# A hardware loop for TensorE's head groups, fixed ring slots, and the last V half in two pieces

## The chip, the cores and the metric

One Trainium2 chip, one core. The metric is the device time of one launch in microseconds, as the median of several runs. On this core most runs of one kernel agree within 0.3%. A ratio is the mean time of one kernel's runs over the mean of the other kernel's runs of the same rounds on the same chip. It is therefore not quite the ratio of the medians that stand beside it. The profile is one execution. Its span runs from the first to the last instruction and is 1.8 to 2.1 us shorter than the time of that run. One run's profile needn't be a median run: the profiled run of the kernel before took 357.92 us.

## The reference

One decode step with two branches that share one input row: grouped-query attention over a cache of 32,768 positions, and a SwiGLU feed-forward. A gate mixes the two.

```python
# x [1,1,512]; 32 query heads, 8 KV heads, head size 128, 32768 cached positions, all bf16
g = sigmoid((x * gate_w).sum(-1))
q = x @ wq                                   # 512 x 4096
scores = q @ k_cache^T * 128 ** -0.5         # k_cache 8 x 32768 x 128
a = (softmax(scores) @ v_cache) @ wo         # v_cache the same size, wo 4096 x 512
b = (silu(x @ w_gate) * (x @ w_up)) @ w_down # 512 x 1792, twice, and back
out = g * a + (1 - g) * b
```

K and V are 64 MiB each. With the weights, 148 MB have to be read, and each byte is used once.

## The kernel before

SP (SyncE) streams everything through a ring of five 4 MB slots in SBUF. Each K or V half of a head group (16,384 positions x 128) is one transfer. Entry i of the stream goes into slot i mod 5, so SP waits until entry i - 5 has been used.

```python
stream = [("wq",), ("K", 0, 0), ("F1",), ("K", 0, 1), ("F2",)]
for g in range(1, G):
    for hf in range(2):
        stream += [("K", g, hf), ("V", g - 1, hf)]
stream += [("V", G - 1, 0), ("V", G - 1, 1), ("wo",)]
place = {e: i for i, e in enumerate(stream)}        # slot = place % 5
...
for i, e in enumerate(stream):                      # SP
    if i >= NSLOT:
        sp.wait_ge(*released[stream[i - NSLOT]])
    ...
        sp.dma_start(dst, src).then_inc(sem_ld[i], 16)
```

PE (TensorE) transposes K tile by tile, as pairs of bf16 read as one fp32. DVE (VectorE) copies every tile from PSUM to SBUF, and PE then multiplies it with q. The maximum, the exponentials and the transposed probabilities follow, and P·V of the group before. PE's program is written out for all eight groups, about 5,300 instructions. All semaphores count upward through the whole kernel.

```python
for e in stream[:-1]:                               # PE
    if e[0] == "K":
        pe.wait_ge(load_sem(e), 16)
        for q in range(FPH):                        # 16 tiles per half
            emit_fill(filled, kv_slot(e), q); filled += 1
            if filled >= NCG * (scored + 1) + 2:
                emit_scores(scored); scored += 1
            ...                                     # transposed P, and O of an earlier group
        continue
    ...
    pe.wait_ge(load_sem(e), 16)
    emit_pv(g, hf, kv_slot(e))
```

DVE's program is written out as well. Its main loop issues up to two waits before each of the 256 tile copies:

```python
for j in range(NF):                                 # DVE, NF = 256
    dve.wait_ge(sem_fill, j + 1)
    if j >= NKT:                                    # NKT = 8 tile buffers, NCG = 4 tiles per score block
        dve.wait_ge(sem_sc, (j - NKT) // NCG + 1)
    dve.tensor_copy(ktT[:, j % NKT, :], pst[j % NST]).then_inc(sem_cp, 1)
    ...
```

After the last V half the tail runs: P·V, a copy, four small matmuls (`osel`; the profile records each as two), scaling, a transposition, and the product with `wo`. `wo` is loaded last, in pieces of 2, 1, 0.5 and 0.5 MB.

## Time and profile before

| | before |
|---|---|
| median time | 357.1 us (later rounds on other chips: 357.4) |
| span of the profiled run | 356.1 us |
| PE / DVE / ACT busy | 72% / 56% / 4% |
| DMA share from 37 to 343 us | 1.00, at 429 GB/s |
| last landing of the last V half / of wo | 342.60 / 352.45 us |

The table by stretches of the kernel before; PEld is PE loading weights, ACT is ScalarE, POOL is GpSimd; the last three columns are the granted PE clock, the DMA share and GB/s:

```profile
core 0: us, PE busy (x) PEld busy (x) DVE busy (x) ACT busy (x) POOL busy (x), PEclk, DMA share, GB/s
37.00:343.00 306.00, 229.68 (x2212) 167.84 (x2214) 180.62 (x324) 13.03 (x34) 2.98 (x8) 0.86 1.00 429
343.00:357.00 14.00, 8.90 (x169) 6.04 (x161) 1.63 (x5) 0.00 (x0) 0.00 (x0) 0.50 0.36 149
```

DMA has no free time between 37 and 343 us, while PE is busy 230 of 306 us. The view of waits agrees: engine, line, whom it waited for; then us in total, times, longest.

```profile
PE ps L415 <- DMA ring<-in_A_k_cache_dram: 59.0, 14, 5.8
PE ps L431 <- DVE ktT L722: 15.1, 16, 0.9
```

PE stands still for K 14 times, up to 5.8 us each. The DMA queues of the page (packets, MB, share of the time of 16 DMA engines):

```profile
q1 hardware_dynamic: 5768, 148.11, 97.2%
q8 instruction: 20, 0.33, 0.4%
q14 instruction: 5, 0.04, 0.0%
```

The page lists q8 and q14 as `instruction` queues: 20 packets of 16 KB and 5 of 8 KB. The records below fit program code of PE and DVE that is fetched piece by piece by some of the DMA engines that also carry K and V, and are read so here. **A transfer lands when the slowest of its sixteen engines is done**: for the last V half the sixteenth update comes at 342.60 us, and PE starts at 342.65. The trace records the semaphore update of each engine for each transfer. Sorted, and with the first one subtracted, they give each engine's distance behind the fastest, in us. These rows are computed from those records; the records don't name the DMA engine:

```
kernel before, 4 MB transfers; first landing at: the sixteen distances
 22.18: 0 .04 .11 .12 .15 .16 .22 .28 .31  .35  .43  .97  1.17 1.20 1.59 1.80
122.51: 0 .05 .20 .28 .34 .94 1.12 1.16 1.50 1.60 1.61 1.67 1.67 1.76 1.84 3.53
229.33: 0 .04 .17 .35 .94 1.13 1.17 1.61 1.68 1.80 3.04 3.15 3.22 3.28 3.38 4.51
326.44: 0 .06 .16 .35 .96 1.16 1.19 3.06 3.11 3.17 3.22 3.23 3.30 4.83 4.95 6.45
```

The fastest engine needs 9.71 us per 4 MB half, from first to last. Eight engines step back one after the other by about 1.45 us, as often as q8 has a packet (16 KB, 1.0 to 1.1 us each). One other engine steps back by about 0.97 us right after each packet of q14 (8 KB; at 50.8, 111.2, 174.1, 243.1 and 307.2 us) and is 6.45 us behind at the end. The q8 packets start every 253 recorded PE instructions on average, those of q14 every 127 recorded DVE instructions. So they are taken for PE's and DVE's programs. The bytes alone, at the 27 GB/s that one engine makes in this stream (4 MB in 9.71 us by sixteen), would be an estimated 0.6 and 0.3 us.

The tail in the chain that ended last (start, us, what):

```profile
342.65 3.62 PE ps L463 x31
346.35 0.70 DVE pv_sb L715
347.09 1.88 PE ps L479 x8
349.98 3.61 PE ps L542 x128
353.73 0.35 DVE res L765
```

### The profile page before, as it was taken

The numbers are of one execution on the slowest core, as the hardware profiler recorded it, in microseconds if no ns is written. First come the engines' busy times: TensorE is split into PE (matmuls) and PEld (weight loads), VectorE is DVE, ScalarE is ACT, GpSimd is POOL, SyncE is SP. The second block draws the span as 40 slices with busy tenths as digits, with TensorE's granted clock in tenths as the row PEclk, the third lists the DMA queues.
The fourth block names the chain that finished last, engine by engine and source line by source line (L and its number), as shares of the span: only waits on it lengthen the run. The fifth ranks groups of instructions, "written<-read, shape, count | busy, mean of one in ns | idle before, by whom it ended". The sixth has DMA issues, their size and how long they took to land.

```text
span 356.1 us, 6079 instructions
## 1 busy us (share of the span) xinstructions
PE 255.3 (72%) x2615; PEld 187.4 (53%) x2615; DVE 197.9 (56%) x371; ACT 14.5 (4%) x36; POOL 5.6 (2%) x22
## 2 busy tenths in 40 slices
PE   0439998849497947858395959778495949577746
PEld 0436885647384726546283838464473728274415
DVE  1239198828266845848183756657282838457401
ACT  1000101000100010000100010000100010000000
POOL 0200000000000000000000000000000000000000
PEclk9999789969859996989789798989698898989555
DMA  8999999999999999999999999999999999999991
GB/s 339 420 405 466 416 431 418 445 429 420 436 438 415 434 436 423 432 438 421 432 436 427 431 429 434 429 421 439 431 418 443 431 414 445 430 420 438 425 380 64
DMA packets 5797, 148.49 MB, mean 417 GB/s; under 512 B 650, under 2 KB 652, under 8 KB 908
## 3 DMA queue, kind: packets, MB, share of 16 engines
q1 hardware_dynamic: 5768, 148.11, 97.2%
q8 instruction: 20, 0.33, 0.4%
q14 instruction: 5, 0.04, 0.0%
q10 hardware_dynamic: 4, 0.00, 0.0%
HBM read 148.11 MB, written 0.00 MB: 416 GB/s over the span
## 4 chain that ended last, share of the span: by engine, by line
DMA 66%; PE 29%; DVE 3%; issue 2%; POOL 0%; SPq 0%; DVEq 0%
DMA ring<-in_A_k_cache_dram 56%; PE ps L415 17%; DMA ring<-in_A_v_cache_dram 10%; PE ps L431 5%; PE ps L463 3%; PE ps L384 2%; DVE ktT L722 2%; PE ps L479 1%; PE ps L542 1%; PE ps L445 0%; DVE pv_sb L715 0%; DVE pmaxf L678 0%; POOL gmax L288 0%; SPq L298 0%; DVE res L765 0%
## 5 line engine op out<-in xcount | busy, mean ns | idle before, releaser
L722 DVE COPY ktT<-ps 128x1024 bf16<-128x1024 bf16 x256 | 163.6, 683 | 104.7 <-PE ps L415 102.0
L415 PE MATMUL ps<-ident_f,ring 128*128 128x128 f32 x1024 | 161.3, 316 | 59.8 <-DMA ring<-in_A_k_cache_dram 59.0
L415 PEld LDWEIGHTS ps<-ident_f,ring 128*128 128x128 f32 x1024 | 136.9, 164 | 93.7 <-DMA ring<-in_A_k_cache_dram 65.7
L431 PE MATMUL ps<-ktT,qz 128*32 128x512 bf16 x512 | 42.1, 406 | 15.2 <-DVE ktT L722 15.1
L463 PE MATMUL ps<-ring,ET 128*16 128x512 bf16 x512 | 33.8, 410 | 5.7 <-DMA ring<-in_A_v_cache_dram 5.5
L463 PEld LDWEIGHTS ps<-ring,ET 128*16 128x16 bf16 x512 | 13.2, 94 | 22.4 <-DMA ring<-in_A_v_cache_dram 5.9
L431 PEld LDWEIGHTS ps<-ktT,qz 128*32 128x32 bf16 x512 | 7.9, 95 | 28.3 <-DVE ktT L722 24.3
L569 ACT ACTIVATE P<-ps,nbias 128x512 bf16<-128x512 f32 x16 | 10.8, 682 | 273.4 <-DVE nbias L699 273.4
L678 DVE TENSOR_REDUCE pmaxf<-ps 128x1 f32<-128x512 f32 x16 | 11.1, 692 | 11.9 <-PE ps L431 11.9
L479 PEld LDWEIGHTS ps<-osel,pv_sb 128*128 128x128 f32 x64 | 11.0, 258 | 2.1 <-DVE pv_sb L715 2.1
L479 PE MATMUL ps<-osel,pv_sb 128*128 128x4 f32 x64 | 10.7, 291 | 1.0 <-DVE pv_sb L715 0.9
L715 DVE COPY pv_sb<-ps 128x512 f32<-128x512 f32 x8 | 5.5, 682 | 8.9 <-PE ps L463 8.9
L288 POOL PARTITION_ALL_REDUCE gmax<-pmax x8 | 3.0, 373 | 310.2 <-DVE pmax L688 310.2
L445 PE MATMUL ps<-ident,P 128*128 128x128 bf16 x64 | 6.2, 219 | 1.8 <-ACT P L569 1.2
L707 DVE COPY ET<-ps 128x512 bf16<-128x512 bf16 x16 | 6.6, 413 | 1.3 <-PE ps L445 1.3
L384 PEld LDWEIGHTS ps<-xT,ring 128*128 128x128 bf16 x112 | 6.8, 159 | 0.4 <-issue 0.4
L384 PE MATMUL ps<-xT,ring 128*128 128x1 bf16 x112 | 6.9, 198 | 0.0
L359 PE MATMUL ps<-xT,ring 128*128 128x1 bf16 x128 | 3.5, 165 | 4.5 <-DMA ring<-in_A_wq_dram 4.5
L445 PEld LDWEIGHTS ps<-ident,P 128*128 128x128 bf16 x64 | 4.8, 98 | 2.6 <-ACT P L569 2.4
L342 PE MATMUL ps<-ones_bf,x_row 1*128 1x1 bf16 x4 | 0.3, 171 | 7.8 <-DMA gw_row<-in_gate_w_dram 7.8
L359 PEld LDWEIGHTS ps<-xT,ring 128*128 128x128 bf16 x128 | 3.5, 104 | 4.5 <-issue 4.5
L342 PEld LDWEIGHTS ps<-ones_bf,x_row 1*128 1x128 bf16 x4 | 0.2, 112 | 7.8 <-DMA gw_row<-in_gate_w_dram 7.8
(67 smaller groups left out, 36.5 us busy)
## 6 DMA issues: line engine op xcount, KB each, us to landing
ring<-in_A_k_cache_dram SPq DMA_DIRECT2D x16, 4096.0 KB, 43.1
ring<-in_A_v_cache_dram SPq DMA_DIRECT2D x16, 4096.0 KB, 37.1
ring<-in_A_wq_dram SPq DMA_DIRECT2D x1, 4096.0 KB, 13.2
ring<-in_A_wo_dram SPq DMA_DIRECT2D x1, 2048.0 KB, 38.8
ring<-in_B_w_gate_dram SPq DMA_DIRECT2D x1, 1792.0 KB, 26.6
ring<-in_B_w_up_dram SPq DMA_DIRECT2D x1, 1792.0 KB, 30.5
ring<-in_B_w_down_dram SPq DMA_DIRECT2D x1, 1792.0 KB, 43.5
ring<-in_A_wo_dram SPq DMA_DIRECT2D x1, 1024.0 KB, 40.8
```

What stands on the lines that cost most here:

```text
L359: ins = pe.matmul(ps_m[:, M_Q0 + h : M_Q0 + h + 1], wq_v[:, c, h * DH : (h + 1) * DH], xT[:, c : c + 1], start=(c == 0), stop=(c == KC - 1),)
L384: ins = pe.matmul(ps_m[:, base + j : base + j + 1], wt[:, c, :].rearrange("d (p j) -> d j p", j=FC)[:, j, :], xT[:, c : c + 1], start=(c = ...
L415: ins = pe.transpose(stb[:, t * 64 : (t + 2) * 64], two.bitcast(FP32), ident_f[:, :])
L431: ins = pe.matmul(ps_sc[f % NSC][32 * c : 32 * c + 32, :], qz[:, g, e, 24 - PB * i : 56 - PB * i], kt[:, e, :], start=(i == 0 and e == 0), ...
L445: ins = pe.transpose(ps_pt[:, (f % 2) * 512 + m * 128 : (f % 2) * 512 + (m + 1) * 128], P[:, f % 2, m * 128 : (m + 1) * 128], ident[:, :],)
L463: ins = pe.matmul(ps_pv[32 * c : 32 * c + 2 * PB, :], ET[:, f % NET, col : col + 2 * PB], src.rearrange("p (i c t) d -> p i c t d", i=NI, ...
L479: ins = pe.matmul(ps_m[:, M_OT + g * HPG : M_OT + (g + 1) * HPG], pv_sb[:, r * DH : (r + 1) * DH], osel[:, r * HPG : (r + 1) * HPG], start ...
L569: act.activation(P[:, f % 2, :], ps_sc[f % NSC], ACT.Exp, bias=nbias[:, f // 2 : f // 2 + 1], scale=SCALE, accum_out=esum[:, f // 2, f % 2 ...
L678: ins = dve.tensor_reduce(pmaxf[:, f : f + 1], ps_sc[f % NSC], AX.X, ALU.max)
L707: dve.tensor_copy(ET[:, f % NET, :], ps_pt[:, (f % 2) * 512 : (f % 2 + 1) * 512]).then_inc(sem_ptc, 1)
L715: dve.tensor_copy(pv_sb[:, :], ps_pv).then_inc(sem_pvc, 1)
L722: dve.tensor_copy(ktT[:, j % NKT, :], pst[j % NST]).then_inc(sem_cp, 1)
```

## The change

Its intent: PE's groups 1 to 7 become one hardware loop, so that its program shrinks, from 5,302 recorded instructions to about 2,020. The loop is written with the same addresses and the same semaphore values in every turn. So K and V halves get fixed slots (four rotate, the fifth holds F2 and later wo), q of the group is copied to one place (`qc`), O of a group is copied out of one PSUM place, and PE subtracts from its semaphores what it has waited for. Besides, the last V half comes as two transfers, so that half of its P·V can run earlier. Cut to its core:

```diff
-    place = {e: i for i, e in enumerate(stream)}
+    place = {("wq",): 1, ("F1",): 3, ("F2",): 4, ("wo",): 4}
+    for g in range(G):
+        for hf in range(2):
+            place["K", g, hf] = 2 * hf
+            place["V", g, hf] = 2 * hf + 1
...   # SP
-                    if i >= NSLOT:
-                        sp.wait_ge(*released[stream[i - NSLOT]])
+                    if e in before:                 # the entry before in the same slot
+                        sp.wait_ge(*released[before[e]])
...
+                        if e == ("V", G - 1, 1):
+                            sp.dma_start(dst[:, : RH // 2, :], src[:, : RH // 2, :]).then_inc(ld, 16)
+                            sp.dma_start(dst[:, RH // 2 :, :], src[:, RH // 2 :, :]).then_inc(sem_ldv, 16)
...   # PE
+                def take(sem, n):
+                    pe.wait_ge(sem, n)
+                    pe.sem_inc(sem, -n)
...
-                for e in stream[:-1]:               # everything written out
-                    ...
+                pe.wait_ge(sem_bpre, 1)
+                with pe.Fori(1, G):
+                    emit_k(0)
+                    emit_pv(0)
+                    emit_k(1)
+                    emit_pv(1)
+                    pe.sem_inc(sem_exp, -2)
+                    pe.sem_inc(sem_ptc, -2)
+                    pe.sem_inc(sem_qc, -1)
...
+                emit_pv(1, halves=True)             # P.V of the first piece, wait for sem_ldv, the rest
...   # DVE: one q copy and one copy of O per group
+                dve.tensor_copy(qc[:, :, :], qz[:, g, :, :]).then_inc(sem_qc, 1)
+                dve.tensor_copy(oT[:, g * HPG : (g + 1) * HPG], ps_m[:, M_OT : M_OT + HPG]).then_inc(sem_oc, 1)
```

More of the change, by code (lines that the diff above doesn't have):

```diff
@@ L71, in bass_gated_mix__gqa_block_cached__swiglu_ffn__decode_kernel @@
     stream += [("V", G - 1, 0), ("V", G - 1, 1), ("wo",)]
-    place = {e: i for i, e in enumerate(stream)}
+    place = {("wq",): 1, ("F1",): 3, ("F2",): 4, ("wo",): 4}
[3 more added lines that the diff above has]
+            place["V", g, hf] = 2 * hf + 1
+    before = {}
+    for i, e in enumerate(stream):
+        for d in stream[:i]:
+            if place[d] == place[e]:
+                before[e] = d
     with ExitStack() as es:
@@ L80, in T @@
             return es.enter_context(nc.sbuf_tensor(name, shape, dt))
-        sem_ld = [S_(f"s_ld{i}") for i in range(len(stream) - 1)]
+        sem_ld = [S_(f"s_ld{i}") for i in range(NSLOT)]
+        sem_ldv = S_("s_ldv")
         sem_ldo = [S_(f"s_ldo{i}") for i in range(len(WO_CUT))]
@@ L122, in bass_gated_mix__gqa_block_cached__swiglu_ffn__decode_kernel @@
         sem_pt = S_("s_pt")
+        sem_qc = S_("s_qc")
+        sem_oc = S_("s_oc")
         sem_ptc = S_("s_ptc")
@@ L163, in bass_gated_mix__gqa_block_cached__swiglu_ffn__decode_kernel @@
         qz = T("qz", [128, G, 2, 56], BF16)
+        qc = T("qc", [128, 2, 56], BF16)
         sg = T("sg", [128, FC], FP32)
@@ L180, in bass_gated_mix__gqa_block_cached__swiglu_ffn__decode_kernel @@
         pv_sb = T("pv_sb", [128, 512], FP32)
+        oT = T("oT", [128, H], FP32)
         oTs = T("oTs", [128, H], BF16)
@@ L201, in bass_gated_mix__gqa_block_cached__swiglu_ffn__decode_kernel @@
         M_OT = M_B0
-        M_O0 = M_OT + H
+        M_O0 = M_OT + HPG
         M_BR = 256
@@ L209, in slot_of @@
         def slot_of(entry):
-            return ring[:, place[entry] % NSLOT, :]
+            return ring[:, place[entry], :]
         def kv_slot(entry):
@@ L294, in _ @@
                 for i, e in enumerate(stream):
-                    if i >= NSLOT:
-                        sp.wait_ge(*released[stream[i - NSLOT]])
+                    ld = sem_ld[place[e]]
+                    if e in before:
+                        sp.wait_ge(*released[before[e]])
                     if e[0] == "wq":
                         sp.dma_start(wq_v, A_wq.rearrange("(p c) n -> p c n", c=KC)).then_inc(
-                            sem_ld[i], 16
+                            ld, 16
                         )
@@ L302, in _ @@
                         sp.dma_start(wg, B_w_gate.rearrange("(p c) f -> p c f", c=KC)).then_inc(
-                            sem_ld[i], 16
+                            ld, 16
                         )
                         sp.dma_start(wu, B_w_up.rearrange("(p c) f -> p c f", c=KC)).then_inc(
-                            sem_ld[i], 16
+                            ld, 16
                         )
@@ L309, in _ @@
                         sp.dma_start(wd, B_w_down.rearrange("(p j) n -> p j n", j=FC)).then_inc(
-                            sem_ld[i], 16
+                            ld, 16
                         )
@@ L325, in _ @@
                         dst = kv_slot(e)
-                        sp.dma_start(dst, src).then_inc(sem_ld[i], 16)
+                        if e == ("V", G - 1, 1):
+                            sp.dma_start(dst[:, : RH // 2, :], src[:, : RH // 2, :]).then_inc(
+                                ld, 16
+                            )
+                            sp.dma_start(dst[:, RH // 2 :, :], src[:, RH // 2 :, :]).then_inc(
+                                sem_ldv, 16
+                            )
+                        else:
+                            sp.dma_start(dst, src).then_inc(ld, 16)
                 sp.wait_ge(sem_res, 1)
@@ L355, in emit_q @@
                 def emit_q():
-                    pe.wait_ge(load_sem(("wq",)), 16)
+                    take(load_sem(("wq",)), 16)
                     for h in range(H):
@@ L379, in emit_ffn @@
                 def emit_ffn():
-                    pe.wait_ge(load_sem(("F1",)), 32)
+                    take(load_sem(("F1",)), 32)
                     for base, wt in ((M_G0, wg), (M_U0, wu)):
@@ L393, in emit_outb @@
                 def emit_outb():
-                    pe.wait_ge(load_sem(("F2",)), 16)
+                    take(load_sem(("F2",)), 16)
                     pe.wait_ge(sem_tT, 1)
@@ L405, in emit_outb, with emit_fill @@
                     ins.then_inc(sem_pe_b, 1)
-                def emit_fill(j, src, q):
-                    if j >= NST:
-                        pe.wait_ge(sem_cp, j - NST + 1)
-                    stb = pst_f[j % NST]
+                def emit_fill(src, q):
+                    stb = pst_f[q % NST]
+                    if q >= NST:
+                        pe.wait_ge(sem_cp, q - NST + 1)
                     for t in range(0, TPF, 2):
@@ L418, in emit_fill, with emit_scores @@
                     ins.then_inc(sem_fill, 1)
-                def emit_scores(b):
-                    f, i = b // NI, b % NI
-                    g = f // 2
-                    if b == 0:
-                        pe.wait_ge(sem_qz, 4)
-                    if i == 0 and f >= NSC:
-                        pe.wait_ge(sem_exp, f - NSC + 1)
-                    pe.wait_ge(sem_cp, NCG * (b + 1))
+                def emit_scores(hf, i, first):
+                    if i == 0 and hf == 0:
+                        pe.wait_ge(sem_qc, 1)
+                    if i == 0 and not first:
+                        pe.wait_ge(sem_exp, hf + 1)
+                    pe.wait_ge(sem_cp, NCG * (i + 1))
                     for e in range(2):
                         for c in range(NCG):
-                            kt = ktT[:, (NCG * b + c) % NKT, :].rearrange("p (k e) -> p e k", e=2)
+                            kt = ktT[:, (NCG * i + c) % NKT, :].rearrange("p (k e) -> p e k", e=2)
                             ins = pe.matmul(
-                                ps_sc[f % NSC][32 * c : 32 * c + 32, :],
-                                qz[:, g, e, 24 - PB * i : 56 - PB * i],
+                                ps_sc[hf][32 * c : 32 * c + 32, :],
+                                qc[:, e, 24 - PB * i : 56 - PB * i],
                                 kt[:, e, :],
@@ L438, in emit_scores, with emit_k, emit_pt @@
                     ins.then_inc(sem_sc, 1)
-                def emit_pt(f):
-                    pe.wait_ge(sem_exp, f + 1)
-                    if f > 0:
-                        pe.wait_ge(sem_ptc, f)
+                def emit_k(hf, first=False):
+                    e = ("K", 0, hf)
+                    take(load_sem(e), 16)
+                    done = 0
+                    for q in range(FPH):
+                        emit_fill(kv_slot(e), q)
+                        if q + 1 >= NCG * (done + 1) + 2:
+                            emit_scores(hf, done, first)
+                            done += 1
+                        if q == NCG and hf == 0 and not first:
+                            emit_o()
+                        if q == FPH // 2 and not first:
+                            emit_pt(hf)
+                    while done < NI:
+                        emit_scores(hf, done, first)
+                        done += 1
+                    pe.sem_inc(sem_cp, -FPH)
+                def emit_pt(hf):
+                    pe.wait_ge(sem_exp, hf + 1)
                     for m in range(NM):
                         ins = pe.transpose(
-                            ps_pt[:, (f % 2) * 512 + m * 128 : (f % 2) * 512 + (m + 1) * 128],
-                            P[:, f % 2, m * 128 : (m + 1) * 128],
+                            ps_pt[:, hf * 512 + m * 128 : hf * 512 + (m + 1) * 128],
+                            P[:, hf, m * 128 : (m + 1) * 128],
                             ident[:, :],
@@ L450, in emit_pt, with emit_pv @@
                     ins.then_inc(sem_pt, 1)
-                def emit_pv(g, hf, src):
-                    f = 2 * g + hf
-                    if hf == 0 and g > 0:
-                        pe.wait_ge(sem_pvc, g)
-                    pe.wait_ge(sem_ptc, f + 1)
-                    for m in range(NM):
-                        for i0 in range(0, NI, 2):
+                def emit_pv(hf, halves=False):
+                    e = ("V", 0, hf)
+                    take(load_sem(e), 16)
+                    pe.wait_ge(sem_ptc, hf + 1)
+                    src = kv_slot(e).rearrange("p (i c t) d -> p i c t d", i=NI, c=NCG)
+                    for i0 in range(0, NI, 2):
+                        if i0 > 0 and halves:
+                            pe.wait_ge(sem_ldv, 16)
+                        for m in range(NM):
@@ L459, in emit_pv @@
                             for c in range(NCG):
                                 col = m * 128 + c * 32 + i0 * PB
-                                first = hf == 0 and m == 0 and i0 == 0
-                                last = hf == 1 and m == NM - 1 and i0 == NI - 2
                                 ins = pe.matmul(
                                     ps_pv[32 * c : 32 * c + 2 * PB, :],
-                                    ET[:, f % NET, col : col + 2 * PB],
-                                    src.rearrange("p (i c t) d -> p i c t d", i=NI, c=NCG)[
-                                        :, i0 : i0 + 2, c, 2 * m : 2 * m + 2, :
-                                    ].rearrange("p i t d -> p i (t d)"),
-                                    start=first,
-                                    stop=last,
+                                    ET[:, hf, col : col + 2 * PB],
@@ L471, in emit_pv, with emit_o @@
+                                    src[:, i0 : i0 + 2, c, 2 * m : 2 * m + 2, :].rearrange(
+                                        "p i t d -> p i (t d)"
+                                    ),
+                                    start=(hf == 0 and i0 == 0 and m == 0),
+                                    stop=(hf == 1 and i0 == NI - 2 and m == NM - 1),
                                 )
                     ins.then_inc(sem_pv, 1)
-                def emit_o(g):
-                    if g == 0:
-                        pe.wait_ge(sem_osel, 1)
-                    pe.wait_ge(sem_pvc, g + 1)
+                def emit_o():
+                    take(sem_pvc, 1)
+                    take(sem_oc, 1)
@@ L478, in emit_o @@
                     for r in range(NBLK):
                         ins = pe.matmul(
-                            ps_m[:, M_OT + g * HPG : M_OT + (g + 1) * HPG],
+                            ps_m[:, M_OT : M_OT + HPG],
                             pv_sb[:, r * DH : (r + 1) * DH],
@@ L490, in _ @@
                 pe.wait_ge(sem_ident, 2)
-                scored = 0
-                filled = 0
-                for e in stream[:-1]:
-                    if e[0] == "K":
-                        pe.wait_ge(load_sem(e), 16)
-                        for q in range(FPH):
-                            emit_fill(filled, kv_slot(e), q)
-                            filled += 1
-                            if filled >= NCG * (scored + 1) + 2:
-                                emit_scores(scored)
-                                scored += 1
-                            if e[1] >= 1 and q == FPH // 2:
-                                emit_pt(2 * (e[1] - 1) + e[2])
-                            if e[2] == 0 and e[1] >= 2 and q == NCG:
-                                emit_o(e[1] - 2)
-                        continue
-                    while scored * NCG < filled:
-                        emit_scores(scored)
-                        scored += 1
-                    if e[0] != "V":
-                        {"wq": emit_q, "F1": emit_ffn, "F2": emit_outb}[e[0]]()
-                        continue
-                    _, g, hf = e
-                    if e == ("V", G - 1, 0):
-                        emit_pt(2 * G - 2)
-                        emit_pt(2 * G - 1)
-                        emit_o(G - 2)
-                    if e == ("V", G - 1, 1):
-                        pe.wait_ge(sem_em, 1)
-                        pe.matmul(
-                            ps_e[:, 0:H],
-                            ones_f[:, :],
-                            em[:, :, :].rearrange("p g h -> p (g h)"),
-                            start=True,
-                            stop=True,
-                        ).then_inc(sem_pe_S, 1)
-                    pe.wait_ge(load_sem(e), 16)
-                    emit_pv(g, hf, kv_slot(e))
@@ L530, in _ @@
-                emit_o(G - 1)
+                pe.wait_ge(sem_osel, 1)
+                emit_q()
+                emit_k(0, first=True)
+                emit_ffn()
+                emit_k(1, first=True)
+                pe.sem_inc(sem_qc, -1)
+                emit_outb()
+                pe.wait_ge(sem_bpre, 1)
[6 more added lines that the diff above has]
+                    pe.sem_inc(sem_ptc, -2)
+                    pe.sem_inc(sem_qc, -1)
@@ new lines, in _ @@
+                emit_pt(0)
+                pe.wait_ge(sem_ptc, 1)
+                emit_pt(1)
+                emit_o()
+                emit_pv(0)
+                pe.wait_ge(sem_em, 1)
+                pe.matmul(
+                    ps_e[:, 0:H],
+                    ones_f[:, :],
+                    em[:, :, :].rearrange("p g h -> p (g h)"),
+                    start=True,
+                    stop=True,
+                ).then_inc(sem_pe_S, 1)
+                emit_pv(1, halves=True)
+                emit_o()
@@ L587, in _ @@
                 dve.memset(ps[:, 6:8, :], 0.0).then_inc(sem_pv0, 1)
+                dve.memset(pv_sb[:, :], 0.0).then_inc(sem_pvc, 1)
+                dve.memset(oT[:, :], 0.0).then_inc(sem_oc, 1)
                 dve.wait_ge(sem_pe_x, 1)
@@ L712, in emit_pvc, with emit_oc, emit_qc @@
                     dve.wait_ge(sem_pv, 2 * (g + 1))
-                    if g > 0:
-                        dve.wait_ge(sem_pe_o, g)
+                    dve.wait_ge(sem_pe_o, g + 1)
                     dve.tensor_copy(pv_sb[:, :], ps_pv).then_inc(sem_pvc, 1)
+                def emit_oc(g):
+                    dve.wait_ge(sem_pe_o, g + 2)
+                    dve.tensor_copy(
+                        oT[:, g * HPG : (g + 1) * HPG], ps_m[:, M_OT : M_OT + HPG]
+                    ).then_inc(sem_oc, 1)
+                def emit_qc(g):
+                    dve.tensor_copy(qc[:, :, :], qz[:, g, :, :]).then_inc(sem_qc, 1)
+                dve.wait_ge(sem_qz, 4)
+                emit_qc(0)
                 for j in range(NF):
@@ L721, in _ @@
                         dve.wait_ge(sem_sc, (j - NKT) // NCG + 1)
-                    dve.tensor_copy(ktT[:, j % NKT, :], pst[j % NST]).then_inc(sem_cp, 1)
+                    dve.tensor_copy(ktT[:, j % NKT, :], pst[q % NST]).then_inc(sem_cp, 1)
                     if j == FPH + 1:
                         emit_t()
-                    if j == 2 * FPH + 1:
-                        emit_bpre()
                     if q == FPH - 1:
@@ L729, in _ @@
                         if f % 2 == 1:
+                            if f < NH - 1:
+                                emit_qc(f // 2 + 1)
                             emit_nbias(f // 2)
@@ L732, in _ @@
                         emit_ptc(f - 2)
+                    if j == 2 * FPH - 1:
+                        emit_bpre()
                     if q == 1 and f >= 4 and f % 2 == 0:
                         emit_pvc(f // 2 - 2)
+                    if q == NCG + 2 and f == 2:
+                        dve.wait_ge(sem_pe_o, 1)
+                        dve.tensor_copy(oT[:, 0:HPG], ps_m[:, M_OT : M_OT + HPG]).then_inc(
+                            sem_oc, 1
+                        )
+                    if q == NCG + 2 and f >= 4 and f % 2 == 0:
+                        emit_oc(f // 2 - 2)
                 emit_ptc(2 * G - 2)
@@ L737, in _ @@
                 emit_ptc(2 * G - 1)
-                dve.wait_ge(sem_exp, NH)
+                emit_oc(G - 2)
                 dchain(
@@ L753, in _ @@
                 emit_pvc(G - 1)
-                dve.wait_ge(sem_pe_o, G)
-                dve.tensor_tensor(oTs[:, :], ps_m[:, M_OT : M_OT + H], rS[:, :], ALU.mult).then_inc(
-                    sem_oT1, 1
-                )
+                dchain(
+                    dve.tensor_tensor(
+                        oTs[:, 0 : H - HPG], oT[:, 0 : H - HPG], rS[:, 0 : H - HPG], ALU.mult
+                    )
+                )
+                dve.wait_ge(sem_pe_o, G + 1)
+                dve.tensor_tensor(
+                    oTs[:, H - HPG :], ps_m[:, M_OT : M_OT + HPG], rS[:, H - HPG :], ALU.mult
+                ).then_inc(sem_oT1, 1)
                 dve.wait_ge(sem_oT1, 1)
```

## The prediction

> **What bounds the kernel now.** The DMA stream. The table by stretches gives a DMA share of 0.98 to 1.01, about 430 GB/s, from 37 to 343 us. PE is busy 72%; between groups it waits for the next K half (waits: 59.0 us in 14 waits, longest 5.8). The trace's landing records (sixteen engines' updates per transfer) say more: the fastest engine finishes a 4 MB half every 9.71 us, while the slowest falls behind, from 1.4 us at the first landing to 6.4 at the last. The steps fit the instruction queues: each 16 KB fetch of PE's program (20 packets, queue q8) costs one engine about 1.45 us, rotating over eight engines, which end up to 4.95 us behind; five 8 KB fetches (q14, which fit DVE's program) all hit one other engine, 0.97 us each: 6.4 us behind. A transfer lands when its slowest engine is done: last V 342.6 us, last wo piece 352.45.
>
> **What the change does.**
> - Tail: in the chain, last V lands at 342.6, then 3.62 us of P·V, 0.70 copy, 1.88 osel matmuls, small steps, wo matmuls 349.98 to 353.6. In two pieces, half of the P·V runs before the last landing: an estimated 1.8 us less, so wo matmuls could start at 348.2. But the last wo piece lands at 352.45, and its 16 matmuls are an eighth of 3.61 us: wo ends at 352.95 instead of 353.6. Only about 0.65 us shows; the rest becomes waiting for wo.
> - Four ring slots rotate instead of five. K's next load is issued when K's transposes end, 10.3 us after landing, and needed 29.1 us after it (three transfers of 9.71): 18.8 us to spare: DMA does not starve. K's issue-to-landing time falls from 43.1 to about 28.5 us.
> - Added: a q copy per group, seven copies of O, a dummy osel product, a wait for b_pre before the loop: inside PE's 4 to 6 us of idle per K half.
> - The loop: about 560 PE instructions per turn[...]. [...] If the loop stays resident, 8 to 10 fetches remain, and PE's engines gain 1.5 to 3 us; but the last landing belongs to DVE's engine, so the time hardly changes. The bad case is refetches always on the same engines: seven on one, about 10.5 us behind, last landing 4 us later.
>
> **Predicted time: 356.7 us, 80% range 355.2 to 360.0.** Chances: faster by over 2% 0.02, within 2% 0.94, slower by over 2% 0.04.
>
> **Right or wrong in the profile.** Last V landing within 0.5 us of 342.6; half of its P·V before it; a wait for wo inside the last matmuls; K landing 28 to 29 us after issue; DMA share 1.00; [...]slowest engine still that of q14's fetches.
>
> **What would make it wrong.** Refetches piling on few engines; [...]a changed number of DVE fetches (0.97 us each).

The time comes to 357.1 us less about 0.4: 0.65 us gained in the tail, less an allowance for some chance of loss. An estimate: 8 to 10 fetches from about 2,020 recorded instructions at one packet per 253, and 10.5 us from seven steps of the measured 1.45 us on top of what an engine is behind at the start.

## The result, and the profile after

| | before | after |
|---|---|---|
| median | 357.1 us (4 runs) | 357.41 us (4 runs) |
| ratio | | 1.0008, 95% interval 0.9991 to 1.0026: the same |
| repeated later, on another chip | 357.47 (11 runs) | 357.29 (5 runs), ratio 0.9993 (0.9980 to 1.0006) |

The queues after:

```profile
q1 hardware_dynamic: 5912, 148.12, 97.3%
q8 instruction: 8, 0.13, 0.2%
q14 instruction: 5, 0.04, 0.0%
```

PE's fetches (q8) fall from 20 to 8; DVE's (q14) stay at five. The last of PE's before the tail ends at 92.6 us, just after the first turn of the loop; the next starts at 349.1. In between, six more turns run without one q8 packet, at 559 recorded PE instructions per turn, where the kernel before had one packet per 253. PE's six taken branches were recorded with 215 to 242 ns each, the one not taken with 83 ns. After each taken branch PE waits 4.3 to 7.7 us for its next K half, and the weight load of its first transposition starts 0.10 us after K has landed, in every turn, as it also does where the same turns are written out (pe_unrolled below). So whatever the branch costs is hidden in the wait for K.

And yet the kernel is no faster. The distances before the gap described below, and at the last V landing:

```
kernel after, first landing at: the sixteen distances
326.41: 0 .03 .10 .17 .18 .24 1.15 1.17 1.42 1.59 1.62 1.77 1.87 1.92 1.96 6.44
338.93: 0 .04 .06 .07 .09 .10 .11 .13 .14 .18 .19 .25 .28 .32 .40 3.71
```

The eight engines that carry PE's program are now at most 1.96 us behind, where they had been up to 4.95. The one that carries DVE's program is 6.44 behind, as before, and it alone sets the landing: 342.64 us instead of 342.60.

The table by stretches for the end, first of the kernel before, then of the kernel after:

```profile
326.00:334.00 8.00, 5.95 (x68) 3.45 (x64) 4.73 (x17) 1.45 (x4) 0.37 (x1) 0.80 0.98 420
```

```profile
326.00:334.00 8.00, 3.97 (x52) 2.18 (x44) 4.30 (x18) 1.45 (x4) 0.37 (x1) 0.93 0.83 328
```

Here the DMA share falls to 0.83, which the prediction had not seen coming. The last V half follows directly on another V half, so its slot (shared with the V half two entries earlier) is needed two transfers later, not four. It was issued at 327.2 us, and fifteen engines had run dry: the first of them finishes the first piece at 334.03 us (331.38 in the run without this gap, see the experiment with the spare slot). The slowest engine had work until 332.85 and lost nothing. That is why the distances shrink from 6.44 to 3.71 without anything getting earlier.

The tail in the timeline (start, us, engine, line, what; in brackets the idle time before and what ended it):

```profile
337.88 1.04 PE L505 MATMUL ps<-ring,ET 128*16 128x512 bf16 x16 [1.04 <-PEq L361]
342.68 1.89 PE L505 MATMUL ps<-ring,ET 128*16 128x512 bf16 x16 [3.76 <-DMA ring<-in_A_v_cache_dram]
348.57 3.46 PE L574 MATMUL ps<-ring,O 128*1 128x128 bf16 x112 [0.28 <-DVE O L819]
352.53 0.59 PE L574 MATMUL ps<-ring,O 128*1 128x128 bf16 x16 [0.50 <-DMA ring<-in_A_wo_dram]
353.30 0.35 DVE L823 SCALAR_TENSOR_TENSOR res<-ps,g_col,b_pre 128x128 bf16<-128x128 f32 x1 [4.78 <-PE ps L574]
```

Half of P·V is done before the last landing, the wo matmuls start at 348.57 instead of 349.98, and then they wait for the last piece of wo (landed 352.49). Of 1.41 us gained at the start, 0.43 is left at the last step (353.30 against 353.73).

A note on reading: after the change, waits for K are no longer listed under DMA. PE now waits in a semaphore instruction of its own, and the view names PE's sequencer:

```profile
PE ps L443 <- PEq L361: 52.1, 14, 6.8
```

### The profile page after: what moved, and what is told of

Its sections match the earlier page's. It is cut to its first block, busy times and chain, and to the rows that moved or that the text cites. A ratio compares the mean times of both kernels' runs of the same rounds, so it can differ in the third digit from the quotient of the medians. Undisturbed runs are those within 1.5% of the kernel's fastest.

```text
span 355.7 us, 6176 instructions
## 1 busy us (share of the span) xinstructions
PE 256.8 (72%) x2623; PEld 187.2 (53%) x2623; DVE 199.8 (56%) x390; ACT 14.5 (4%) x36; POOL 5.6 (2%) x22
## 5 line engine op out<-in xcount | busy, mean ns | idle before, releaser
L443 PEld LDWEIGHTS ps<-ident_f,ring 128*128 128x128 f32 x1024 | 135.3, 163 | 87.5 <-issue 61.2
L457 PE MATMUL ps<-ktT,qc 128*32 128x512 bf16 x512 | 42.6, 410 | 15.2 <-DVE ktT L766 15.1
L505 PE MATMUL ps<-ring,ET 128*16 128x512 bf16 x512 | 33.0, 401 | 6.7 <-DMA ring<-in_A_v_cache_dram 3.8
L457 PEld LDWEIGHTS ps<-ktT,qc 128*32 128x32 bf16 x512 | 7.9, 95 | 28.8 <-DVE ktT L766 24.3
L520 PEld LDWEIGHTS ps<-osel,pv_sb 128*128 128x128 f32 x72 | 13.0, 270 | 3.0 <-issue 3.0
L520 PE MATMUL ps<-osel,pv_sb 128*128 128x4 f32 x72 | 12.6, 299 | 1.7 <-PEq L361 1.7
L574 PE MATMUL ps<-ring,O 128*1 128x128 bf16 x128 | 4.1, 307 | 0.8 <-DMA ring<-in_A_wo_dram 0.5
## 6 DMA issues: line engine op xcount, KB each, us to landing
ring<-in_A_k_cache_dram SPq DMA_DIRECT2D x16, 4096.0 KB, 26.5
```

The source lines that it names most:

```text
L443: ins = pe.transpose(stb[:, t * 64 : (t + 2) * 64], two.bitcast(FP32), ident_f[:, :])
L457: ins = pe.matmul(ps_sc[hf][32 * c : 32 * c + 32, :], qc[:, e, 24 - PB * i : 56 - PB * i], kt[:, e, :], start=(i == 0 and e == 0), stop=(i ...
L505: ins = pe.matmul(ps_pv[32 * c : 32 * c + 2 * PB, :], ET[:, hf, col : col + 2 * PB], src[:, i0 : i0 + 2, c, 2 * m : 2 * m + 2, :].rearrang ...
L520: ins = pe.matmul(ps_m[:, M_OT : M_OT + HPG], pv_sb[:, r * DH : (r + 1) * DH], osel[:, r * HPG : (r + 1) * HPG], start=(r == 0), stop=(r = ...
```

## The experiments

The theory: the end is set by the one DMA engine that carries DVE's program; TensorE's loop relieves engines that were not last; and the split of V turns into a wait for wo. The rivals: the loop's saving was real and was lost to the gap in the stream; branches cost what fetches saved; or DVE's program doesn't matter at all. Each timed run is set against the kernel before on the same chip (357.36, 357.48 and 357.47 us in the three groups).

All results together. "Behind" is the slowest engine's distance at the V half that lands from 326.4 us on; landings are those of the slowest engine.

| kernel | q8 / q14 packets | behind | last V | last wo | last step | median | ratio to before |
|---|---|---|---|---|---|---|---|
| before | 20 / 5 | 6.45 | 342.60 | 352.45 | 353.73 | 357.4 | 1 |
| after | 8 / 5 | 6.44 | 342.64 | 352.49 | 353.30 | 357.41 | 1.0008 |
| changed_again | 7 / 5 | 6.09 | 342.39 | 352.30 | 353.46 | 357.29 | 0.9993 |
| pe_unrolled | 21 / 5 | 6.21 | 342.46 | 352.36 | 352.97 | 357.12 | 0.9989 |
| loop_spare_slot | 8 / 5 | 5.79 | 342.05 | 351.88 | 352.69 | 357.42 | 1.0001 |
| loop_whole_v | 8 / 5 | 5.93 | 342.15 | 351.99 | 353.63 | 357.70 | 1.0007 |
| before_split_v | 20 / 5 | 5.76 | 342.04 | 351.88 | 352.48 | 357.14 | 0.9989 |
| loop_long_dve | 8 / 6 | 6.96 | 343.19 | 353.20 | 354.01 | 358.32 | 1.0022 |
| loop_longer_dve | 7 / 7 | 8.16 | 344.51 | 354.49 | 356.10 | 359.98 | 1.0066 |
| before_short_dve | 20 / 4 | 4.92 | 341.01 | 350.85 | 351.45 | 356.09 | 0.9965 |
| loop_short_dve | 8 / 3 | 4.32 | 340.56 | 350.40 | 351.20 | 355.77 | 0.9960 |
| dve_loop_only | 21 / 1 | 4.87 | 341.06 | 351.02 | 351.83 | 356.15 | 0.9963 |
| both_loops | 8 / 1 | 2.50 | 338.74 | 348.61 | 349.42 | 353.73 | 0.9897 |
| both_loops_spare | 8 / 1 | 2.36 | 338.64 | 348.50 | 349.31 | 353.39 | 0.9884 |

The intervals are ±0.0012 to ±0.0018 (±0.4 to ±0.6 us). A run's "behind" contains 1.3 to 2.2 us that engines already differ by in the first 22 us, and this part changes by some tenths from run to run. Differences under 0.5 us between single profiles are therefore not read as effects.

### A shorter DVE program: loop_short_dve and before_short_dve

```diff
-                    if j >= NKT:
+                    if q >= NKT and q % NCG == 0:
                         dve.wait_ge(sem_sc, (j - NKT) // NCG + 1)
...
-                    if f >= NET:
-                        dve.wait_ge(sem_pv, f - NET + 1)
```

The waits left out are implied by earlier ones: three of four repeat a value, others are covered by the wait before the maximum, and those on P·V by PE's order. Both kernels gave correct results. In the looped kernel the recorded DVE instructions fall from 668 to 438; no work changes.

> The changed kernel, with 230 of DVE's waits left out that an earlier wait already implies (216 on the score counter, 14 on the P.V counter), so that its program is about 440 recorded instructions long instead of 668. Theory (the end is set by the one DMA engine that carries DVE's program fetches): three q14 fetches in the span instead of five, slowest engine about 4.5 us behind instead of 6.44, last V landing about 1.9 us earlier (near 340.7), time 1.5 to 2.1 us below the changed kernel's. Rival (the loop's saving was lost to the late last V load, or the time is set elsewhere): fewer fetches, but time within 0.5 us of the changed kernel.

> The kernel before, with the same waits left out of DVE's program. Theory: three q14 fetches, DVE's engine about 4.5 us behind; now the engines with three PE fetches are last, 4.95 us behind. So the last V lands about 1.5 us earlier than before (near 341.1) and the time falls by 1.0 to 1.6 us, a little less than the looped kernel with the same cut. Rival: no change.

Queues of loop_short_dve, then of before_short_dve (one of its four q14 packets starts at 0.1 us, at the very start of the span):

```profile
q8 instruction: 8, 0.13, 0.2%
q14 instruction: 3, 0.02, 0.0%
```

```profile
q8 instruction: 20, 0.33, 0.4%
q14 instruction: 4, 0.02, 0.0%
```

Leaving out 230 waits that waited for nothing moves the last V landing from 342.64 to 340.56 us and the time to 355.77 us, 1.6 us under the changed kernel. In the kernel before, the same edit gives 356.09. There DVE's engine is 4.6 us behind, and the last engines are now those with three PE fetches (4.7 to 4.9 us). The theory's numbers hold for both; the rivals expected no change.

### A longer DVE program: loop_long_dve and loop_longer_dve

```diff
+                    if q == FPH // 2:
+                        for _ in range(FPH):        # loop_longer_dve: range(36)
+                            dve.wait_ge(sem_xT, 2)  # reached long ago
```

> The changed kernel, with 256 waits on a counter that was reached long ago added to DVE's program, 16 per half[...]. Theory: two more q14 fetches (seven), slowest engine about 8.4 us behind, last V landing and time 1.9 us later than the changed kernel. Rival: DVE has slack, so no change in time.

> The changed kernel with 36 waits of no effect added to DVE's program in each half (the 16 of the earlier run showed as 8 recorded instructions, so some 288 more in all). Theory: seven q14 fetches instead of five, last V landing and time 1.5 to 2.1 us later than the changed kernel. Rival: DVE has slack, so no change.

The first run missed in size: 16 such waits became 8 recorded instructions, so there was one fetch more (six), not two. The time rose by 0.9 us over the spare-slot run of the same chip, which is one fetch's worth. The second run had seven fetches. Its last V landed 2.1 us after that of the changed kernel on the same chip, as expected, and its time rose by 2.7 us, 0.6 more than expected. The excess is in the tail: from the last V landing to the last step it takes 11.59 us, against 11.07 in changed_again. Of these 0.52 us, a longer pause before the last 18 matmuls (to 0.76 us past the landing of wo instead of 0.56; see the end of this section) makes 0.2 and slower matmuls after it (0.70 us instead of 0.44) 0.26. DVE does have slack (it is busy 56% of the span in the kernel after), and it does not help, because the cost falls on the DMA engine.

### The spare slot: loop_spare_slot

```diff
+    place["V", G - 1, 1] = 4          # idle through the loop
+    place["wo",] = 3
```

> The changed kernel, but the last V half goes into the ring slot that lay idle through the loop, and wo into the slot it leaves, so that its load is issued about 20 us earlier. Theory: the 2.7 us gap of fifteen engines before the last V half goes away (their last landings come 2.7 us earlier) but the slowest engine never ran dry, so the last V still lands near 342.6 and the time stays within 0.4 us. Rival (the loop's saving was lost to this gap): 2 to 2.7 us faster than the changed kernel.

The gap is gone (table by stretches of this run; compare 0.83 and 328 GB/s above):

```profile
326.00:334.00 8.00, 5.10 (x72) 2.75 (x68) 4.78 (x18) 1.45 (x4) 0.37 (x1) 0.96 0.99 420
```

The first landing of the first piece is back at 331.38 us. The time is 357.42 us. So the loop's saving was not lost to the gap; that rival falls.

### The split of V alone, and left out: before_split_v and loop_whole_v

> The changed kernel with the last V half loaded and used whole, as before. Theory (the wo landing near 352.5 ends the kernel, so the split is worth only what the last wo piece leaves): last V landing unchanged near 342.6, wo matmuls start near 350 instead of 348.6 and do not wait for wo, wo ends 0.4 to 0.8 us later, time up by as much. Rival (the split's 1.8 us counts in full): 1.5 us or more slower than the changed kernel.

> The kernel before with the split of the last V half alone. Theory: last V landing unchanged, half of its P.V done before it, wo matmuls start about 1.4 to 1.8 us earlier and then wait for the last wo piece; time 0.3 to 0.7 us below before. Rival (the split needs the loop, or counts in full): no change, or 1.5 us faster.

The edits are the two `dma_start` calls and the wait on `sem_ldv` shown in the diff, put into the kernel before (with the order of P·V's two loops turned round, as the change has it too) or taken out of the changed one. As expected, the wo matmuls start earlier after the last V landing with the split (5.67 us in before_split_v, 5.93 in the changed kernel) than without (7.38 and 7.73), and then wait for the last piece of wo. From the last V landing to the last step, the kernel before takes 11.13 us and loop_whole_v 11.48; with the split, before_split_v takes 10.44 and the changed kernel 10.66. So by these profiles the split saves 0.7 to 0.8 us after the landing, with the loop or without, not 1.8; against the second profile of the changed kernel (changed_again, 11.07) only 0.4 is left. Neither change of the median (-0.34 us for the split alone, +0.3 to +0.4 without it) is outside its interval.

### The loop alone, left out: pe_unrolled

```diff
-                with pe.Fori(1, G):
+                for _ in range(1, G):
```

> The changed kernel itself, once more, to stand beside the next three on one chip: near 357.4 us, ratio to before 0.998 to 1.002.

> The changed kernel with TensorE's seven turns written out instead of looped: the same instructions, slots, copies and semaphores taken back, without the branch. Theory: q8 fetches rise again from 8 to about 20 or 21, the engines that carry them end up to 4.9 us behind, but DVE's engine is 6 us or more behind in both, so the last V landing and the time stay within 0.5 us of the changed kernel. Rival (the loop saves time, or its branch costs some): a difference of 1 us or more in either direction.

```profile
q8 instruction: 21, 0.34, 0.4%
q14 instruction: 5, 0.04, 0.0%
```

With all 21 fetches back, three of the engines are 4.72 to 4.90 us behind again, and the time is 357.12 against 357.29 us: no difference. In this kernel the hardware loop itself is worth nothing and costs nothing, within the ±0.5 us of the intervals.

### Both loops: both_loops, both_loops_spare, dve_loop_only

DVE's groups 1 to 7 become a loop of 53 recorded instructions per turn. Its semaphores are taken back at the end of a turn; its results go to single places; the q and O copies, whose addresses change from group to group, go to ACT; SP releases K slots by a counter of DVE's own.

```diff
-                for j in range(NF): ...
+                emit_group(True)
+                with dve.Fori(1, G):
+                    emit_group(False)
...
+                        if g < G - 1:               # ACT
+                            act.copy(qc[:, :, :], qz[:, g + 1, :, :]).then_inc(sem_qc, 1)
```

> The changed kernel with DVE's groups 1 to 7 in a hardware loop too, the implied waits left out, and the q and O copies moved to ACT[...]. Theory: one or two q14 fetches in the span instead of five, DVE's engine at most about 2.6 to 3.5 us behind; the gap before the late last V load (2.7 us on the other engines) now counts, last V lands near 339.3 to 339.6, time 2.8 to 3.4 us below the changed kernel. Rival: no better than the short DVE program (355.8).

> The same, with the last V half in the ring slot that lies idle through the loop, so that no engine runs dry before it. Theory: the slot, which was worth nothing to the changed kernel, is worth 0.3 to 0.8 us here; last V lands near 338.5 to 338.9, time 3.2 to 3.9 us below the changed kernel, near 353.7. Rival: same time as both_loops.

> The kernel with both loops and the spare slot, but with TensorE's turns written out. Theory: with DVE's fetches gone, TensorE's count: about 20 q8 fetches, one q14, slowest engine about 4.9 us behind, last V landing near 341.1, time 2.0 to 2.8 us above the kernel with both loops (353.4), so near 355.8. Rival (TensorE's loop is worth nothing): the same time as with both loops.

Queues of both_loops_spare, then of dve_loop_only, which differs from it in PE's loop alone:

```profile
q8 instruction: 8, 0.13, 0.2%
q14 instruction: 1, 0.01, 0.0%
```

```profile
q8 instruction: 21, 0.34, 0.4%
q14 instruction: 1, 0.01, 0.0%
```

The tail of both_loops_spare in the timeline, to be set against that of the changed kernel:

```profile
338.69 1.88 PE L510 MATMUL ps<-ring,ET 128*16 128x512 bf16 x16 [3.75 <-DMA ring<-in_A_v_cache_dram]
344.60 3.30 PE L579 MATMUL ps<-ring,O 128*1 128x128 bf16 x110 [0.28 <-DVE O L829]
349.31 0.35 DVE L833 SCALAR_TENSOR_TENSOR res<-ps,g_col,b_pre 128x128 bf16<-128x128 f32 x1 [4.77 <-PE ps L579]
```

The same steps run 4.0 us earlier. Both loops with the spare slot give 353.39 us, ratio 0.9884 (0.9869 to 0.9899), the best kernel; all runs were correct. Write PE's turns out again and 2.8 us are lost (356.15): **the loop that was worth nothing in the change is worth 2.8 us once the other engine's fetches are gone.** Against the kernel before, DVE's loop without PE's (with slots and split) gives only 1.3 us, PE's without DVE's nothing; both together give 4.1. A maximum over engines behaves so.

One expectation fell. I had thought that the gap before the last V half would now count and that the spare slot would be worth 0.3 to 0.8 us. But both_loops has no gap: its first piece lands first at 331.35 us without the spare slot, and its last V lands at 338.74 us instead of the expected 339.3 to 339.6. With the engines closer together the last K half lands 3.9 us earlier (309.53 us; 313.42 in the changed kernel). PE's work on it, the P·V that follows and frees the slot, and the issue of the last V half (323.29 instead of 327.18) all come earlier by as much. So the gap itself had come from the slow engine. The two medians differ by 0.34 us, within their intervals.

### A pause of PE near a q8 packet

In several looped kernels PE pauses 18 matmuls before the end of its work, whether their data is there or not. The timeline of changed_again:

```profile
348.33 3.36 PE L574 MATMUL ps<-ring,O 128*1 128x128 bf16 x110 [0.28 <-DVE O L819]
352.86 0.44 PE L574 MATMUL ps<-ring,O 128*1 128x128 bf16 x18 [1.17 <-issue]
```

The first two of these 18 belong to a piece of wo that had landed at 351.06, and the rest to one that landed at 352.30; they start at 352.86, 0.56 us after their data. A q8 packet ended at 351.35 us. In six of these kernels the pause ends 1.3 to 1.5 us after the end of such a packet, and the wait falls at the same instruction. In the first profile of the changed kernel the packet ended at 350.38 us, 1.2 us earlier when both are counted from the start of the wo matmuls, and the pause cost nothing. No experiment moved the packet, so this is an observation and not a tested cause.

## Why the prediction was right

- **Time.** Predicted 356.7 us, range 355.2 to 360.0; measured 357.41 and, repeated, 357.29. The class "within 2%" and the range hold. The gain of 0.4 us that it meant (0.65 less some chance of loss) did not show clearly: the two measurements stand 0.08% above and 0.07% below before, within their intervals.
- **What bounds the kernel.** Right. It named the slowest DMA engine, not the average share of DMA, and DVE's program on it. The experiments that lengthen and shorten DVE's program show it: with PE's loop, 3, 6 and 7 q14 packets give last V landings of 340.56, 343.19 and 344.51 us, and the seven profiles with 5 packets, with the loop or without, lie between 342.04 and 342.64.
- **The loop.** Of its cases, the one that it calls "stays resident" came true: 8 fetches, none of them between 92.6 and 349.1 us. For that case it said that the time would hardly change; writing the loop out left the time the same (pe_unrolled). Which case would come true it left open.
- **The branch.** The case of more fetches did not occur: of the six taken branches, from 91.4 to 287.3 us, only the first has a q8 packet near it (at 91.6 us). Whether a stall at a branch would have been hidden stays untested; PE has 4.2 to 7.6 us between the end of a branch and the next landing.
- **The tail.** Right in mechanism: half of P·V early, then a wait for wo. In the first profile wo ended about as early as computed: the last 16 matmuls began at 352.53, 0.04 us after the landing. They and the step after took longer than the estimate of 0.45 us (0.59 us for the 16), so 0.43 us was left of the 0.65. In the second profile a further 0.56 us went to PE's pause before its last 18 matmuls, which the prediction didn't have.
- **"DMA does not starve".** This step was wrong at one place. In the steady alternation of K and V there is time to spare, as it said (about 17 us rather than 18.8, with the K time of the next point), but at the end two V halves follow one another, and the last one's slot came free too late: DMA share 0.83 from 326 to 334 us. It cost nothing, as loop_spare_slot shows, because only the engines that were ahead ran dry. The prediction had not worked this out, so here it was lucky.
- **K from issue to landing.** Predicted 28 to 29 us, measured 26.5 (median). The 10.3 us taken for K's transposes is the shortest of the sixteen halves in the profile before: with `osel` matmuls between them they take 12.3 to 15.0 us, without 10.3 to 12.6. Four transfers of 9.71 us less the measured 26.5 leave 12.3 us.

## What to carry to other kernels

When DMA is the bound, ask for the slowest of the sixteen engines, not for the mean: the landing records show how far each one is behind, and small transfers that always fall on one engine count there: here five 8 KB packets, 0.97 us each, on the engine that was 6.45 us behind. Removing a cost that wasn't on the last engine changed nothing here (357.29 us with PE's loop, 357.12 without), and is worth keeping in mind for when the last one is dealt with: two changes worth 0 and 1.3 us alone (each with the slots and the split) were worth 4.1 together. Count the program's instructions, redundant waits included, on every engine; leaving out waits that an earlier wait implies is the cheapest gain (1.6 us under the changed kernel).
